# A list scheduler that plans three engines learns of a port that two of them share

## The chip, the cores and the metric

One core of one Trainium2 chip runs the whole program. The metric is the device time of one execution in microseconds, the median of three runs. TensorE is PE in the profile, VectorE is DVE, ScalarE is ACT, GpSimd is POOL, and SyncE (SP) issues the DMAs.

## What is computed

Three layers follow one another, all in float32 (a_re, a_im, q, k, v are 4 x 8 x 768 x 48):

```python
# 1: a linear attention with complex decay, per head, step by step over 768 positions
S_re, S_im = ar * S_re - ai * S_im + k v^T, ar * S_im + ai * S_re
y[t] = q[t] @ S_re
# 2: an MLP 384 -> 2048 -> 384 on 3072 tokens with a rational activation P(h) / Q(h)
g = (a0 + a1*h + a2*h2 + a3*h3) / (1 + |b0|*|h| + |b1|*h2 + 1e-6);  x = g @ w_out
# 3: a mixture of 8 experts 384 -> 1024 -> 384, all tokens through all experts,
#    weighted by P, a softmax normalised 8 times over rows and columns
out += P[:, e:e+1] * (max(x @ w1[e], 0) @ w2[e])
```

## The kernel before

The program has two parts. The **first part** (layers 1 and 2) is a list schedule made at build time; the **second part** (layer 3, `second_mlp`, L1298, and `experts`, L1004) is written out in a fixed order: 384 steps of 9 and 12 matmuls, with one ACT and one DVE instruction between the two.

Layer 1 is cut into 13 pieces. For each piece `attn_normalise` (L345) computes the decay, `attn_prefix` (L385) multiplies it up over the piece (tiles f1a, f2a, u, tot, x, ex), `attn_scale` (L486) scales q and k by it (tiles f1, f2, an, kq) and writes them to a scratch in DRAM, and `attn_unit` and `attn_half` (L534, L582) read them back (tile raw) for 128 tokens at a time, transpose them on PE, multiply and mask them, and give xt, the input of layer 2. Layer 2 works on 12 tiles of 256 tokens and 8 groups of weights: `moe1_first` (L783) does 18 matmuls (h) and the rational function (tiles m, gt, gh, gl) on ACT and DVE, and `moe1_second` (L827) multiplies by the second weights (tile x, results x2s).

Each of these functions is a generator that yields operations. An `Op` (L93) knows its engine, its estimated duration (`cost`) and its inputs: `self.ins` (L101) holds the operands except those that are the very same object as the output. So `scalar_tensor_tensor(out=s1, in0=s1, scalar=c, in1=s3, ...)` of `moe1_first` has s3 and the small c in `ins`, and not s1.

Many two-operand products are an `Either` (`g.tt`): DVE and POOL can both do them, and the planner takes the one with the lower start + cost x (1 + PRICE). With the costs of L93 to L123, a product of 384 columns is 0.468 us on DVE and 0.956 us on POOL.

`Schedule.run` (L300) is the planner. It holds one time per engine at which it is free (`free_at`), finds the operation that can start first, and among the operations of that engine that can start then takes the one whose stream has the earliest due date. It emits that operation and sets the engine's time. The due dates (L1416 to L1430) are multiples of PITCH for each tile of tokens, of GROUP for each group of weights, less a lead for each kind of work: OA for the prefix, ON for the normalising, OB for the scaling, OU for the units, OW for the weights; OS is a lag. All instructions of an engine, and all DMAs of SP's queue, are issued in the order in which the planner emitted them, and semaphores keep the data right, so durations that the planner has wrong change the times on the chip and not the result.

Of the kernel before, what the change touches and what calls it, by code (L numbers as in the profile page):

```python
# [15 lines left out]
PSUM, DRAM = bass.MemoryType.PSUM, bass.MemoryType.DRAM  # L16
# [45 lines left out]
PLAIN = 'FFFSSFFS'  # L62
SMP = 'DD'

PITCH = 52.78
GROUP = 5.87
OU = 61.28
OB = 99.68
OA = 215.64
ON = 87.12  # L70
OW = 36.95
OS = 26.64
SLACK = 0
HHD = 2.38
SH = (-2.5, 27.9, -15.0, 1.6, 3.1, -26.5, 4.2, 13.7, 4.0, 12.5, -36.2, -58.1, 17.9)
WS = 1.91
PRICE = {'DVE': 1.78, 'POOL': 0.13, 'ACT': -0.39}
LAT = {'PE': 0.2, 'ACT': 0.145, 'DVE': 0.13, 'POOL': 0.075, 'SP': 1.0}
TS = True

# [12 lines left out]
class Op:  # L93


    def __init__(self, eng, fn, args, kw):
        self.eng, self.fn, self.args, self.kw = eng, fn, args, kw
        self.deps = []
        self.out = kw["out"] if "out" in kw else args[0]
        ap = [x for k, x in [*enumerate(args), *kw.items()] if k not in ("out", "accum_out", "op", "func") and hasattr(x, "tensor")]  # L100
        self.ins = [x for x in ap if x is not self.out]  # L101
        n = int(np.prod(self.out.shape[1:]))
        ps = any(x.space == PSUM for x in self.ins)
        name = fn.__name__
        ptr = sum(hasattr(kw.get(k), "tensor") for k in ("scale", "bias", "accum_out", "scalar")) + (
            name == "tensor_scalar" and sum(hasattr(x, "tensor") for x in args[2:4]))
        self.lat = LAT[eng]
        if eng == "PE":
            f32 = args[1].dtype != F32R
            two = f32 and not kw.get("is_transpose")  # L110
            self.cost = (1 + two) * max(n * (1 + f32) / 2400, 0.108)
            if two:
                self.cost = {32: 0.076, 96: 0.162}.get(self.out.shape[0], self.cost)
        elif eng == "ACT":
            self.cost = (0.05 if ps else 0.092) + n * 0.836e-3 + 0.0935 * ptr
        elif eng == "DVE":
            one = name == "tensor_scalar" and not ps
            self.cost = ((n / 2 if one else n) + 65) / 960 + 0.061 * ptr
        elif eng == "POOL":
            c = {"tensor_tensor": 2.1, "tensor_scalar": 1.18, "affine_select": 0.9}.get(name, 0.8)  # L120
            self.cost = (0.15 if c > 0.8 else 0.04) + c * n * 1e-3
        else:
            self.cost = 0.06  # L123
# [55 lines left out]
def extent(ap):  # L179

    dims = list(ap.ap)
    o = ap.offset
    if ap.space != DRAM:
        o %= dims[0][0] or 1
        dims = dims[1:]
    return ap.tensor.name, o, o + sum((n - 1) * abs(s) for s, n in dims) + 1


class Schedule:


    def __init__(self, bufs):
        self.bufs = bufs
        self.free_at = dict.fromkeys(("PE", "DVE", "ACT", "POOL", "SP", "DGE", "DMA"), 0.0)
        self.streams, self.seen, self.queues, self.of, self.base = [], {}, {}, {}, {}
        self.log = []

# [13 lines left out]
    def resume(self, s, val):  # L211
        while True:
# [13 lines left out]
            else:  # L226
                if isinstance(x, Either):
                    s.head = [([op], self.ready([op]), op.cost * (1 + PRICE[op.eng])) for op in x.ops]
                else:
# [39 lines left out]
    def ready(self, ops):  # L269
# [7 lines left out]
                        op.deps.append(ix)  # L277
        return r

    def emit(self, s, ops, start):  # L280
        f = self.free_at
        for op in ops:
            if op.eng == "SP":
                f["SP"] = start + op.cost
                t = f["DGE"] = max(f["DGE"], start) + 0.55
                t = f["DMA"] = max(f["DMA"], t + 0.65) + int(np.prod(op.out.shape)) * 4 / 360e3
                end = t + op.lat
                start = f["SP"]
            else:
                end = start + op.cost  # L290
                f[op.eng] = start = end
                end += op.lat
            ins = op.fn(*op.args, **op.kw)  # L293
            self.log.append((op.eng, start - op.cost if op.eng != "SP" else t - 0.5, end, ins, op))
            for ap, w in [(op.out, True)] + [(x, False) for x in op.ins]:
                n, a, b = extent(ap)
                self.seen.setdefault(n, []).append((a, b, end, w, op.eng, len(self.log) - 1))
        self.resume(s, None)

    def run(self):  # L300
        while self.streams:
            go = True
            while go:
                go = False
                for s in sorted((s for s in self.streams if s.wait is not None), key=lambda s: s.key):
                    if s.wait is not None and self.grant(s):
                        go = True
            best = None
            for s in self.streams:
                if s.head is None:  # L310
                    continue
                ops, r, _ = min(s.head, key=lambda h: max(h[1], self.free_at[h[0][0].eng]) + h[2])
                e = ops[0].eng
                t = max(r, self.free_at[e])
                if best is None or t < best[0]:
                    best = t, s, ops, e
            if best is None:
                if self.streams:
                    raise RuntimeError("nothing can go on: " + "; ".join(
                        f"{s.gen.__name__} {s.key:.0f}: {[y.kw['name'] for y in (s.wait if isinstance(s.wait, list) else [s.wait])] if not callable(s.wait) else s.gen.gi_frame.f_lineno}" for s in self.streams)[:400])  # L320
                return
            t0, _, _, e = best
            pick = None
            for s in self.streams:
                if s.head is None:
                    continue
                ops, r, _ = min(s.head, key=lambda h: max(h[1], self.free_at[h[0][0].eng]) + h[2])
                if ops[0].eng != e:
                    continue
                t = max(r, self.free_at[e])  # L330
                if t <= t0 + SLACK and (pick is None or (s.key, t) < pick[0]):
                    pick = (s.key, t), s, ops, t
            self.emit(pick[1], pick[2], pick[3])
# [200 lines left out]
def attn_unit(g, p, u, due):  # L534
# [24 lines left out]
    for hh in range(2):  # L559
        g.add(attn_half(g, n, t0 == 0, last, raw[hh], vt, hh), due + hh * HHD)  # L560
    yield lambda: ("H", n, 0) in g.done and ("H", n, 1) in g.done
# [265 lines left out]
def moe1_second(g, m):  # L827
# [3 lines left out]
    for gi in range(NG):  # L831
        yield lambda: (m, gi) in g.gs and (2 * gi, 1) in g.w1 and (2 * gi + 1, 1) in g.w1
        yield m * PITCH + gi * GROUP + OS
        gh, gl = g.gs.pop((m, gi))
# [451 lines left out]
def x2_load(g, t):  # L1286

    per = TB // TK
    yield lambda: all(("S", t * per + i) in g.done for i in range(per))
    xt = yield New(g.px[t], [128, 2, 3, TB], F32R, keep=True, tag=f"x{t}", name=f"xb{t}")  # L1290
    for l in range(2):
        yield g.eng[4].dma_start(
            out=xt[:, l].bitcast(F32), in_=g.x2g[l, :, :, t * TB:(t + 1) * TB].rearrange("k p t -> p k t")
        )
    g.x2[t] = xt
# [21 lines left out]
def kernel_body(tc, g):  # L1317
# [77 lines left out]
    def tail():  # L1395
# [8 lines left out]
        for t in range(4):  # L1404
            sch.add(x2_load(g, t), PITCH * NT // TK)
        for n in range(8):
            sch.add(expert_entry(g, n), PITCH * NT // TK + n)

    with tc.manual_schedule():
# [4 lines left out]
        for p in range(NP):  # L1414
            b, t0, st = PIECES[p]
            due = PITCH * ((b * S + t0) // TK) + (p == 1) + SH[p]  # L1416
            for hf in range(st // 8):
                sch.add(attn_normalise(g, p, hf), due - ON)
            sch.add(attn_prefix(g, p), due - OA)
            for s in range(st // 4):  # L1420
                sch.add(attn_scale(g, p, s), due - OB)
            for u in range(st // 8):
                sch.add(attn_unit(g, p, u, due - OU + u), due - OU + u)
        for f in range(NF):
            for i in range(2):
                sch.add(moe1_weights(g, f, i), f * WS * GROUP / 2 - OW + i * OS)
        for m in range(NT // TK):
            for gi in range(NG):
                sch.add(moe1_first(g, m, gi), m * PITCH + gi * GROUP)
            sch.add(moe1_second(g, m), m * PITCH + OS)  # L1430
        sch.add(tail(), 0)
# [47 lines left out]
```

## Time and profile before

| | us |
|---|---|
| median of 3 runs (2558.86 to 2560.88) | 2558.94 |
| the profiled execution | 2555.27 |
| its span, first to last instruction | 2553.4 |
| PE busy | 2331.3 |
| DVE busy | 1219.5 |
| ACT busy | 859.3 |
| POOL busy | 662.8 |

The profile page divides the span in 40 slices. In the first 14 of them, some 900 us, all four engines work; in the others PE is busy nearly all the time and the others little. The first matmul `he` of the second part begins at 901 us. An instruction's duration in the profile contains the time in which it has started and cannot get on.

### The profile page before, as it was taken

The page shows a single profiled execution, that of the slowest core. Times are in us where ns is not written, and L with a number is a line of the kernel's source. Part 1 is how long each engine was busy: PE and PEld are TensorE (multiplying, and loading weights), DVE is VectorE, ACT ScalarE, POOL GpSimd, SP SyncE. Part 2 cuts the span into 40 slices and gives each one's busy share as a digit, 9 for nine tenths or more (in the row PEclk, how much of TensorE's full clock was granted, in tenths as well). Part 3 has the DMA queues.
Part 4 walks back from the last instruction along what each step waited for, and adds up shares of the span by engine and source line. Part 5 has one row for each costly group of instructions (what it writes and reads, how often), then busy time and mean ns, then how long its engine had stood idle before and what let it go on. Part 6 is the DMA issues. An engine that isn't in the chain of part 4 may idle for free.

```text
span 2553.4 us, 34934 instructions
## 1 busy us (share of the span) xinstructions
PE 2331.3 (91%) x13921; PEld 2100.8 (82%) x13921; DVE 1219.5 (48%) x2093; ACT 859.3 (34%) x1752; POOL 662.8 (26%) x728
## 2 busy tenths in 40 slices
PE   0468888788899999999999999999999999999998
PEld 0357777777789988999998998998998999999998
DVE  7998989999766633442233224224222222222222
ACT  3456666666667741131121121111112112112111
POOL 5776777777630120020020020011002002001000
PEclk9888999988999999999999999999999999999999
DMA  4533323233320430020021011002001001000000
GB/s 131 161 91 110 95 86 108 86 104 98 107 88 23 155 124 1 1 87 7 1 68 32 1 44 56 1 19 81 1 1 50 1 1 50 1 1 19 25 25 27
DMA packets 141839, 138.20 MB, mean 54 GB/s; under 512 B 32480, under 2 KB 126688, under 8 KB 141664
## 3 DMA queue, kind: packets, MB, share of 16 engines
q1 hardware_dynamic: 141664, 135.86, 17.1%
q8 instruction: 111, 1.82, 0.3%
q14 instruction: 64, 0.52, 0.1%
HBM read 102.80 MB, written 33.03 MB: 53 GB/s over the span
## 4 chain that ended last, share of the span: by engine, by line
PE 71%; DVE 8%; POOL 4%; issue 3%; DMA 2%; ACT 1%; SPq 0%; POOLq 0%; DVEq 0%
PE ye L1035 10%; PE ye L1036 10%; PE he L664 10%; PE ye L1037 10%; PE he L663 10%; PE he L665 10%; PE x L293 4%; PE h L293 3%; DVE m L293 2%; POOL an L293 1%; DVE f L293 1%; POOL kq L293 1%; DVE n L293 1%; DVE f1a L293 1%; ACT m L293 1%
## 5 line engine op out<-in xcount | busy, mean ns | idle before, releaser
L1023 DVE SCALAR_TENSOR_TENSOR lo<-he,hi 128x512 fp32r<-128x512 f32 x384 | 265.4, 691 | 1100.9 <-ACT hi L1022 1100.8
L1022 ACT ACTIVATE hi<-he 128x512 fp32r<-128x512 f32 x384 | 229.7, 598 | 1201.9 <-PE he L665 1055.2
L293 DVE SCALAR_TENSOR_TENSOR m<-m,co,m 128x512 f32<-128x512 f32 x192 | 172.3, 925 | 25.0 <-ACT m L293 24.7
L293 ACT ACTIVATE m<-m,co 128x512 f32<-128x512 f32 x192 | 137.3, 719 | 1.4
L293 PE MATMUL t<-cst_sb,raw 128*96 128x128 f32 x384 | 64.4, 297 | 34.4 <-DMA raw<-kqd 26.8
L1048 DVE SCALAR_TENSOR_TENSOR acc<-ye,skp,acc 128x384 f32<-128x384 f32 x168 | 92.2, 611 | 5.7 <-PE ye L1037 2.4
L293 DVE SCALAR_TENSOR_TENSOR m<-m,co,h 128x512 f32<-128x512 f32 x96 | 71.0, 740 | 34.9 <-ACT m L293 34.7
L293 PEld LDWEIGHTS t<-cst_sb,raw 128*96 128x96 f32 x384 | 46.6, 138 | 43.2 <-issue 24.0
L293 PE MATMUL sh<-tot,cst_sb 128*128 128x96 f32 x26 | 8.1, 408 | 76.4 <-DVE tot L293 73.4
L293 PE MATMUL sc<-tt,tt 96*128 96x128 f32 x384 | 59.7, 304 | 18.9 <-ACT tt L293 17.3
L293 PEld LDWEIGHTS sc<-tt,tt 96*128 96x128 f32 x384 | 53.5, 212 | 24.7 <-ACT tt L293 20.1
L293 POOL TENSOR_TENSOR gl<-m,gh 128x512 fp32r<-128x512 f32 x31 | 44.3, 1431 | 111.2 <-ACT gh L293 111.2
L293 PEld LDWEIGHTS sh<-tot,cst_sb 128*128 128x128 f32 x26 | 5.7, 274 | 79.2 <-POOL tot L293 51.1
L293 ACT ACTIVATE m<-h,co 128x512 f32<-128x512 f32 x96 | 65.4, 681 | 12.3 <-DVE gt L293 6.8
L293 ACT ACTIVATE m<-h 128x512 f32<-128x512 f32 x96 | 56.6, 590 | 32.4 <-PE h L293 32.2
L293 ACT COPY tt<-t 96x512 f32<-96x512 f32 x95 | 54.2, 574 | 28.5 <-PE t L293 28.1
L293 POOL TENSOR_TENSOR f<-an,ex 128x384 f32<-128x384 f32 x51 | 62.5, 1232 | 4.2 <-DVE ex L293 4.1
L293 ACT ACTIVATE m<-m 128x512 f32<-128x512 f32 x96 | 60.2, 628 | 1.3
L293 POOL TENSOR_TENSOR kq<-an,f 128x384 f32<-128x384 f32 x39 | 47.2, 1209 | 36.5 <-DVE f L293 31.3
L293 POOL TENSOR_TENSOR an<-f,f 128x192 f32<-128x192 f32 x61 | 48.9, 811 | 12.8 <-DVE f L293 12.4
L293 DVE SCALAR_TENSOR_TENSOR gt<-m,m 128x512 f32<-128x512 f32 x60 | 50.9, 849 | 2.3 <-PE x L293 0.5
L293 ACT ACTIVATE n<-n,bias 128x384 f32<-128x384 f32 x72 | 43.7, 608 | 10.0 <-POOL n L293 5.9
(1329 smaller groups left out, 7134.6 us busy)
## 6 DMA issues: line engine op xcount, KB each, us to landing
rawe<-in_moe_w SPq DMA_DIRECT2D x128, 192.0 KB
kqd<-kq SPq DMA_DIRECT2D x48, 384.0 KB
raw<-kqd SPq DMA_DIRECT2D x48, 384.0 KB
x2g<-x2s SPq DMA_DIRECT2D x36, 256.0 KB
xb<-x2g SPq DMA_DIRECT2D x12, 768.0 KB
raw<-in_moe_w_in SPq DMA_DIRECT2D x48, 128.0 KB
raw<-in_moe_w_out SPq DMA_DIRECT2D x16, 384.0 KB
rawc<-in_moe_w_in SPq DMA_DIRECT2D x16, 384.0 KB
```

The costliest lines, as they stand in the source:

```text
L293: ins = op.fn(*op.args, **op.kw)
L663: pe.matmul(out, w[0], x[0], start=start, stop=False, **kw),
L664: pe.matmul(out, w[0], x[1], start=False, stop=False, **kw),
L665: pe.matmul(out, w[1], x[0], start=False, stop=stop, **kw),
L1022: act.activation(hi, ps, AF.Relu)
L1023: v.scalar_tensor_tensor(out=lo, in0=ps, scalar=0.0, in1=hi.bitcast(F32), op0=ALU.max, op1=SUB)
L1035: pe.matmul(ys[j], hi[:, c], wh, start=f == 0, stop=False)
L1036: pe.matmul(ys[j], hi[:, c], wl, start=False, stop=False)
L1037: pe.matmul(ys[j], lo[:, c], wh, start=False, stop=f == NFE - 1)
L1048: v.scalar_tensor_tensor(out=acc, in0=ys[j], scalar=g.P[:, i, e:e + 1], in1=acc, op0=MULT, op1=ADD)
```

## The change

The planner gets one more resource, PORT, with a time at which it is free. An operation of POOL that reads SBUF, and an operation of DVE that has two inputs in SBUF or is a `tensor_scalar` or `tensor_copy` from SBUF, starts no earlier than PORT is free, and holds PORT for its whole estimated duration. Inputs are counted from `ins`. The planner's duration of a matmul of rounded operands grows by 0.013 us. PITCH, GROUP, the leads, two of the 13 shifts SH by more than a unit, and the three values of PRICE are new. No operation is added or taken away, pools and buffers stay as they are, and the second part is the same text.

```diff
-PITCH = 52.78
-GROUP = 5.87
-OU = 61.28
-OB = 99.68
-OA = 215.64
-ON = 87.12
-OW = 36.95
-OS = 26.64
+PITCH = 63.96
+GROUP = 6.92
+OU = 52.54
+OB = 77.92
+OA = 199.64
+ON = 97.15
+OW = 45.47
+OS = 27.91
-HHD = 2.38
-SH = (-2.5, 27.9, -15.0, 1.6, 3.1, -26.5, 4.2, 13.7, 4.0, 12.5, -36.2, -58.1, 17.9)
+HHD = 2.39
+SH = (-2.5, 31.7, -15.0, 20.1, 3.1, -26.5, 4.2, 13.7, 4.0, 12.5, -36.2, -58.5, 17.9)
-PRICE = {'DVE': 1.78, 'POOL': 0.13, 'ACT': -0.39}
+PRICE = {'DVE': 1.0, 'POOL': 0.05, 'ACT': -0.18}
...
+        sb = sum(x.space != PSUM and int(np.prod(x.shape[1:])) > 1 for x in self.ins)
+        self.port = sb > 0 and (eng == "POOL" or eng == "DVE" and (sb > 1 or not ps and name in ("tensor_scalar", "tensor_copy")))
...
-            self.cost = (1 + two) * max(n * (1 + f32) / 2400, 0.108)
+            self.cost = (1 + two) * max(n * (1 + f32) / 2400, 0.108) + 0.013 * (not f32)
...
-        self.free_at = dict.fromkeys(("PE", "DVE", "ACT", "POOL", "SP", "DGE", "DMA"), 0.0)
+        self.free_at = dict.fromkeys(("PE", "DVE", "ACT", "POOL", "SP", "DGE", "DMA", "PORT"), 0.0)
...
+    def start(self, h):
+        t = max(h[1], self.free_at[h[0][0].eng])
+        return max(t, self.free_at["PORT"]) if h[0][0].port else t
+
...
                 f[op.eng] = start = end
+                if op.port:
+                    f["PORT"] = end
...
-                ops, r, _ = min(s.head, key=lambda h: max(h[1], self.free_at[h[0][0].eng]) + h[2])
+                h = min(s.head, key=lambda h: self.start(h) + h[2])
+                ops, t = h[0], self.start(h)
```

## Rows read from the trace of the kernel before

**Rows 1.** Five stretches: us; busy PE, PEld, DVE, ACT, POOL; PE's clock; DMA share, GB/s

```profile
0.00:128.00 128.00, 32.53 (x202) 27.02 (x206) 106.75 (x231) 53.87 (x131) 84.21 (x103) 0.90 0.48 146
128.00:448.00 320.00, 252.05 (x2130) 225.21 (x2122) 289.88 (x462) 207.38 (x456) 234.17 (x262) 0.91 0.33 98
448.00:704.00 256.00, 212.18 (x1776) 192.07 (x1777) 225.18 (x382) 160.78 (x352) 179.30 (x208) 0.92 0.32 97
...
768.00:901.00 133.00, 132.88 (x1099) 125.30 (x1099) 86.38 (x125) 96.65 (x189) 18.87 (x15) 1.00 0.25 86
901.00:2553.40 1652.40, 1643.67 (x8196) 1476.75 (x8194) 469.21 (x830) 300.62 (x546) 121.09 (x120) 1.00 0.09 28
```

**Rows 2.** DVE's groups by shape, 128 to 704 us: count, busy us, mean ns, idle before

```profile
L293 DVE SCALAR_TENSOR_TENSOR m<-m,co,m 128x512 f32<-128x512 f32 x124 | 119.0, 983 | 4.3 <-ACT m L293 4.2
L293 DVE SCALAR_TENSOR_TENSOR m<-m,co,h 128x512 f32<-128x512 f32 x62 | 45.7, 737 | 1.5 <-ACT m L293 1.3
L293 DVE SCALAR_TENSOR_TENSOR gt<-m,m 128x512 f32<-128x512 f32 x38 | 35.3, 930 | 0.5 <-DVE m L293 0.5
L293 DVE TENSOR_TENSOR f<-an,ex 128x384 f32<-128x384 f32 x37 | 32.9, 899 | 1.8 <-POOL kq L293 1.8
L293 DVE SCALAR_TENSOR_TENSOR n<-n,n 128x384 f32<-128x384 f32 x38 | 30.5, 803 | 4.8 <-ACT n L293 3.1 <-POOL n L293 1.3
L293 DVE TENSOR_TENSOR f1a<-an 128x384 f32<-128x384 f32 x26 | 25.3, 973 | 1.8 <-POOL an L293 1.8
...
L293 DVE SCALAR_TENSOR_TENSOR f<-f,runs,k 128x192 f32<-128x192 f32 x40 | 21.2, 530 | 5.5 <-ACT f L293 5.4
L293 DVE SCALAR_TENSOR_TENSOR m<-m,m 128x512 f32<-128x512 f32 x23 | 19.7, 855 | 0.0
L293 DVE TENSOR_TENSOR an<-f,f 128x192 f32<-128x192 f32 x27 | 18.7, 700 | 0.0
...
L293 DVE COPY g<-u 96x192 f32<-96x192 f32 x6 | 2.1, 344 | 0.0
L293 DVE TENSOR_TENSOR u<-an 128x96 f32<-128x96 f32 x7 | 1.9, 296 | 1.0 <-POOL an L293 1.0
```

**Rows 3.** Timeline, 564 to 568 us, DVE and POOL: start us, us

```profile
564.14 0.99 POOL L293 TENSOR_TENSOR kq<-an,q 128x384 f32<-128x384 f32 x1
...
565.24 0.68 DVE L293 SCALAR_TENSOR_TENSOR gt<-m,m 128x512 f32<-128x512 f32 x1
...
566.13 0.60 POOL L293 TENSOR_TENSOR f<-f 128x192 f32<-128x192 f32 x1
...
566.70 0.28 POOL L293 TENSOR_TENSOR tot<-u,u 128x48 f32<-128x48 f32 x1
...
566.86 0.20 DVE L293 TENSOR_TENSOR tot<-u,u 128x48 f32<-128x48 f32 x1
566.94 1.00 POOL L293 TENSOR_TENSOR n<-n,n 128x384 f32<-128x384 f32 x1
566.98 1.37 DVE L293 SCALAR_TENSOR_TENSOR n<-n,n 128x384 f32<-128x384 f32 x1
```

**Rows 4.** Timeline, 311 to 314 us, DVE: start us, us

```profile
311.73 0.55 DVE L293 TENSOR_TENSOR kq<-an,q 128x384 f32<-128x384 f32 x1
312.20 0.35 DVE L293 TENSOR_TENSOR f<-f 128x192 f32<-128x192 f32 x1
...
313.16 0.42 DVE L293 SCALAR_TENSOR_TENSOR f<-f,runs,k 128x192 f32<-128x192 f32 x1
```

**Rows 5.** POOL's groups by shape, 128 to 704 us, columns as in rows 2

```profile
L293 POOL TENSOR_TENSOR f<-an,ex 128x384 f32<-128x384 f32 x43 | 53.3, 1248 | 2.8 <-DVE ex L293 2.7
L293 POOL TENSOR_TENSOR an<-f,f 128x192 f32<-128x192 f32 x53 | 42.8, 818 | 12.8 <-DVE f L293 12.4
...
L293 POOL TENSOR_TENSOR x<-u,u 128x48 f32<-128x48 f32 x56 | 26.1, 479 | 41.2 <-DVE u L293 41.2
```

**Rows 6.** PE's longest wait, 0 to 128 us: total us, times, longest

```profile
PE sh L293 <- DVE tot L293: 52.5, 3, 35.4
```

More of the change, by code (lines that the diff above doesn't have):

```diff
@@ L311, in run @@
                     continue
-                ops, r, _ = min(s.head, key=lambda h: max(h[1], self.free_at[h[0][0].eng]) + h[2])
+                h = min(s.head, key=lambda h: self.start(h) + h[2])
+                ops, t = h[0], self.start(h)
                 e = ops[0].eng
-                t = max(r, self.free_at[e])
                 if best is None or t < best[0]:
@@ L326, in run @@
                     continue
-                ops, r, _ = min(s.head, key=lambda h: max(h[1], self.free_at[h[0][0].eng]) + h[2])
+                h = min(s.head, key=lambda h: self.start(h) + h[2])
+                ops, t = h[0], self.start(h)
                 if ops[0].eng != e:
                     continue
-                t = max(r, self.free_at[e])
                 if t <= t0 + SLACK and (pick is None or (s.key, t) < pick[0]):
```

## The prediction

> **What bounds the kernel now.** I read the page first: its slices show four busy engines up to about 900 us and PE alone after that. So I cut the span into stretches [rows 1]. From 901 us on PE is busy 1643.67 of 1652.4 us at full clock; the change does not touch that part, and nothing can be won there. From 768 to 901 us PE is busy 132.88 of 133 us: a backlog of layer 2 is drained. Before that PE is not the bound: it idles 95.5 us in the first 128, and between 128 and 704 us it is busy 464 of 576 us, at a granted clock of 0.91 to 0.92 of 2.4 GHz. In those 576 us DVE is busy 515 and POOL 413. I take DVE, with 61 us idle, as the engine whose pace counts there.
>
> Then I read DVE's groups in that stretch [rows 2]. Two forms of one operation and one size stand side by side: `m<-m,co,h`, one of whose inputs is in PSUM, takes 737 ns; `m<-m,co,m`, with both in SBUF, takes 983. The timeline shows why [rows 3]. A POOL product of 48 columns starts at 566.70 and takes 0.28 us, and DVE meets nothing. At 566.94 POOL starts a product of 384 columns, 1.00 us, at 566.98 DVE starts one, and DVE's takes 1.37 us, where 0.55 us is enough [rows 4]: 0.96 us of POOL, then its own. DVE and POOL take turns at something when both read SBUF.
>
> **How much is waiting.** Own durations by width, unhindered: on DVE 0.55 us for 384 columns, 0.35 for 192, 0.42 for the three-operand one of 192 [rows 4], 0.68 for 512 and 0.20 for 48 [rows 3], 0.737 for the `m` form with a pointer [rows 2]; on POOL 0.99, 0.60 and 0.28 for 384, 192 and 48 [rows 3]. DVE's waits: `m<-m,co,m` 124 x (983 - 737) ns = 30.5 us, `gt` 38 x 250 = 9.5, `f` 37 x 349 = 12.9, `n` 38 x 253 = 9.6, `f1a` 26 x 423 = 11.0, `f<-f,runs,k` 40 x 110 = 4.4, `m<-m,m` 23 x 175 = 4.0, together 82; the 19 smaller groups from `an<-f,f` to `u<-an`, taken the same way, give 70 [rows 2]. So 152 of DVE's 515 us are waiting, 363 its own. Eleven groups with a PSUM input, `m<-m,co,h` to the copy `g<-u`, hold 109 of the 363 (124 by the rows, less 0.057 us for each of 260 instructions: groups overlap by that much). The other 254 us need the shared port. POOL's waits are 43 x 258 ns = 11.1, 53 x 218 = 11.6, 56 x 199 = 11.1 [rows 5], and 57 in its 18 other groups: 91 of 413, so 322 of its own. The two demands, 254 + 322 = 576 us, are as long as the stretch. **The port is taken all the time**; that is the bound.
>
> **What the change moves.** No instruction is added or removed. Three things happen.
>
> First, the planner stops laying two port users over one another, where it sees them. It does not see all. It counts inputs from `ins`, and `ins` leaves out the operand that is also the output, so the in-place DVE forms count one input: `m<-m,co,m` (88 us of its own), `m<-m,m` (16), `f<-f,runs,k` (17), half of `n<-n,n` (10) and some small ones, 126 of the 254 us after overlap. It sees 128.
>
> The row says that these forms wait like the others (983 against 737 ns) [rows 2]. The Trainium skill, page "SBUF — State Buffer", section "Who interferes with whom", says the same against this change: a DVE instruction with two SBUF inputs contends with a GpSimd instruction that reads SBUF, and the second to start is blocked entirely; it makes no exception for an input that is overwritten. If the in-place forms were free, as the plan has it, the sum below would be 64 us of gain and not 42.
>
> Second, work goes from POOL to DVE. With equal starts a product of 384 columns scored 0.468 x 2.78 = 1.30 on DVE against 0.956 x 1.13 = 1.08 on POOL, and POOL took it; now it is 0.94 against 1.00, and DVE does. POOL starts alone only while DVE does something that the plan takes for port-free: 109 + 126 = 235 of 363 us, 65%. So I let POOL keep two thirds: a third, 107 us, goes over and costs DVE 0.55 x 107 = 59 us. (None and all are the ends.)
>
> The new length of the stretch has two bounds. If the port stays full and nothing else limits, it is 254 + 59 + 215 = 528 us, 48 less. If the waits only shrink with POOL's share, to 101 us, and DVE's 61 idle us stay, it is 363 + 59 + 101 + 61 = 584 us, 8 more. The plan then sees (128 + 59) of (254 + 59) us, 60%, and I weigh by that: 0.6 x (-48) + 0.4 x 8 = **-26 us**. In the first 128 us PE's longest wait is for DVE's `tot`, 52.5 us [rows 6], in the same contest (DVE 107, POOL 84 us busy); at the same rate, 128 x 26 / 576, that is **-6 us**, between 0 and twice that.
>
> Third, the dates. In tiles of tokens (leads divided by PITCH) the prefix's lead falls from 4.09 to 3.12, the scaling's from 1.89 to 1.22, the units' from 1.16 to 0.82: attention runs less far ahead, and layer 2 comes earlier in the middle, where PE idles 44 us between 448 and 704. The drain of 133 us, in which DVE has 47 us free and POOL 114 [rows 1], gets shorter by what PE did before. I take a quarter of the 44, **-10 us**, between 0 (layer 2 waits for DVE as before) and -22. The new PE duration changes no matmul, only dates. SP's queue is reordered with the work: a load behind a store of kq that waits for a later kq comes later too. I cost that at nothing, since the DMA engines are a third busy [rows 1] and every lead stays above 45 us; if the cover is gone it is part of the upper end.
>
> **Sum:** -26 - 6 - 10 = -42 us. The profiled execution is 2555.27 us (span 2553.4 and 1.9 around it), 3.7 below the median, so I apply it to the median: 2558.94 - 42 = **2517 us**.
>
> **Rivals.** (a) The plan is too blind. It now puts POOL on purpose beside the in-place `m` forms, which hold the port, so that what the seen forms save is lost again there. For it: half of the demand is unseen. Against it: the plan of before saw none. The 26 and 6 us fall to 0 to 10, the 10 to 0 to 10, and a lost wait adds up to 3: 2535 to 2562 us.
>
> (b) Slower: DVE becomes the bound. With DVE's surcharge cut, everything goes over: 363 + 0.55 x 322 + 61 idle = 601 us, 25 more, and 6 more at the start: 2590 us. It decides from where 177 us x the share moved plus the waits left exceeds 152; at a third moved that is 93 us of waits, at two thirds 34. For it: DVE has only 61 us of slack now. Against it: DVE's waits must go with POOL's work, and as long as DVE is in an operation that the plan takes for free, POOL gets the next product.
>
> (c) The plan's seen half is worth all of the first bound, with half of POOL's work moved: 576 - 0.45 x 161 = 504, 72 us less, and 16 elsewhere: 2471 us. PE then has 464 us of work in 504, which is still less.
>
> **How the numbers follow.** Forecast (2472 to 2535): 0.62; rival (a): 0.20; rival (b): 0.14; beyond (c): 0.04. 0.2%, about 5 us, is what a measurement of this kernel can tell from no change. Of (a) some 0.09 lies below 2554, 0.09 within the 5 us and 0.02 above. Faster: 0.62 + 0.04 + 0.09 = 0.75; same 0.09; slower 0.14 + 0.02 = 0.16. The range 2471 to 2562 holds the forecast and (a), 0.82.
>
> **What would show it.** Right: in the new profile POOL has a fourth to a half fewer two-operand products and DVE that many more; DVE's `f`, `f1a`, `an` and `tot` come down towards 0.55, 0.35 and 0.20 us, while `m<-m,co,m` stays above 0.9; the first `he` comes about 42 us before 901; PE idles less between 128 and 704 us, and the drain before `he` is shorter. The stretch after `he` keeps its 1652 us. Wrong: `m<-m,co,m` rises above 1.1 us (then it is (a)); DVE has over 560 us of its own in the stretch, with POOL mostly idle (then (b)); or PE waits for the tile raw or for loads in place of DVE, which would be the queue.

## The result and the profile after

The changed kernel takes 2520.89 us (median of four runs, 2518.48 to 2526.12) against 2558.90 of the kernel before on the same chip: a ratio of 0.9854, 95% interval [0.9837, 0.9871]. 2517 was forecast, in a range of 2471 to 2562. The profiled execution takes 2521.8 us, its span is 2519.8. The medians differ by 38.0 us and the two profiled executions by 33.5; what follows accounts for the latter. The first matmul `he` of the second part starts at 866.7 us, before at 901.2.

Four stretches, up to that matmul and after it (columns as in rows 1):

```profile
0.00:128.00 128.00, 36.68 (x269) 30.72 (x270) 97.41 (x276) 53.50 (x129) 42.96 (x54) 0.91 0.42 125
128.00:704.00 576.00, 490.87 (x4141) 444.49 (x4140) 512.14 (x980) 387.22 (x843) 288.37 (x326) 0.92 0.34 101
704.00:866.70 162.70, 157.55 (x1323) 146.75 (x1321) 123.25 (x209) 113.85 (x226) 38.60 (x46) 0.99 0.35 112
866.70:2519.80 1653.10, 1643.41 (x8195) 1476.64 (x8193) 468.21 (x834) 299.50 (x544) 113.86 (x113) 1.00 0.09 28
```

The second part keeps its length: 1653.1 us, before 1652.2. All that is gained lies ahead of it. PE's idle time in the first 128 us goes from 95.5 to 91.3; from 128 to 704 us from 111.8 to 85.1; from there to `he` from 6.2 to 5.2; and PE's busy time up to `he` from 687.8 to 685.1. Together 4.2 + 26.7 + 1.0 + 2.7, within rounding the 34.5 us by which `he` comes earlier. POOL is busy 288 us in the long stretch, where it was 413 [rows 1]; DVE starts 980 instructions there, where it was 843, and is busy 512 us, where it was 515.

DVE's groups from 128 to 704 us (count, busy us, mean ns, idle before), to be held against rows 2:

```profile
L302 DVE SCALAR_TENSOR_TENSOR m<-m,co,m 128x512 f32<-128x512 f32 x136 | 119.6, 911 | 7.9 <-ACT m L302 7.9
L302 DVE SCALAR_TENSOR_TENSOR m<-m,co,h 128x512 f32<-128x512 f32 x68 | 49.9, 737 | 0.4 <-ACT m L302 0.3
L302 DVE SCALAR_TENSOR_TENSOR gt<-m,m 128x512 f32<-128x512 f32 x43 | 34.0, 792 | 0.1
L302 DVE TENSOR_TENSOR f<-an,ex 128x384 f32<-128x384 f32 x52 | 32.6, 643 | 0.0
...
L302 DVE SCALAR_TENSOR_TENSOR m<-m,m 128x512 f32<-128x512 f32 x25 | 23.3, 933 | 0.3
...
L302 DVE TENSOR_TENSOR an<-f,f 128x192 f32<-128x192 f32 x36 | 14.2, 405 | 0.0
...
L302 DVE TENSOR_TENSOR f1a<-an 128x384 f32<-128x384 f32 x23 | 12.9, 561 | 0.0
```

And POOL's, against rows 5:

```profile
L302 POOL TENSOR_TENSOR an<-f,f 128x192 f32<-128x192 f32 x36 | 28.3, 789 | 19.6 <-DVE f L302 19.5
L302 POOL TENSOR_TENSOR x<-u,u 128x48 f32<-128x48 f32 x51 | 26.7, 541 | 30.7 <-DVE u L302 30.7
...
L302 POOL TENSOR_TENSOR f<-an,ex 128x384 f32<-128x384 f32 x20 | 24.3, 1222 | 12.6 <-ACT n L302 8.4 <-DVE ex L302 3.6 <-ACT ex L302 0.6
```

The forms that the plan now sees have lost most of their wait (how much of that is due to the plan, the experiments show): `f1a` took 973 ns on average and takes 561, `an<-f,f` 700 and now 405, `f<-an,ex` 899 and now 643. The in-place forms still wait: `m<-m,co,m` 911 ns beside 737 for its twin with a PSUM input, and `m<-m,m` has gone up, from 855 to 933. 136 of the `m<-m,co,m` fit into the stretch and not 124: layer 2 is further on. POOL does `f<-an,ex` 20 times where it did it 43 times, and each still takes 1.2 us.

**An account of the first part.** For every kernel of this study the same sum is made over all instructions of DVE and POOL ahead of the first `he`: for each group of one operation, tiles and shape, its count times its shortest instruction is its own time, and what its instructions took beyond that is waiting. "Port" is the own time of POOL's products and of DVE's forms with two SBUF inputs, in place or not, or with the SBUF form of `tensor_scalar` or copy. Instructions overlap a little, so own time and waiting add up to more than the busy time, and the port's column is an upper figure.

| kernel | instructions in the page, DVE / POOL | port us | DVE own us | DVE waits us | first he at us |
|---|---|---|---|---|---|
| before | 2093 / 728 | 872 | 620 | 209 | 901 |
| changed | 2295 / 537 | 803 | 709 | 120 | 867 |

DVE does 202 instructions more; its own work grows by 89 us, and its waits shrink by as much. The port is needed 69 us less.

### The profile page after: what moved, and what is told of

The parts are those of the page before. It is cut to its first block, busy times and chain, and to the rows that moved or that the text cites. A ratio compares the mean times of both kernels' runs of the same rounds, so it can differ in the third digit from the quotient of the medians.

```text
span 2519.8 us, 34763 instructions
## 1 busy us (share of the span) xinstructions
PE 2328.5 (92%) x13921; PEld 2098.6 (83%) x13921; DVE 1201.0 (48%) x2295; ACT 854.1 (34%) x1741; POOL 483.8 (19%) x537
## 4 chain that ended last, share of the span: by engine, by line
PE 74%; DVE 11%; DMA 6%; issue 3%; POOL 3%; ACT 3%; SPq 1%; POOLq 0%; DVEq 0%; ACTq 0%
PE ye L1044 10%; PE ye L1045 10%; PE ye L1046 10%; PE he L673 10%; PE he L672 10%; PE he L674 10%; PE x L302 4%; DVE m L302 3%; PE h L302 3%; DVE f L302 1%; DMA ai<-in_a_im 1%; ACT m L302 1%; PE t L302 1%; PE sc L302 1%; DVE n L302 1%
## 5 line engine op out<-in xcount | busy, mean ns | idle before, releaser
L302 DVE SCALAR_TENSOR_TENSOR m<-m,co,m 128x512 f32<-128x512 f32 x192 | 165.5, 894 | 18.7 <-ACT m L302 18.5
L302 PE MATMUL t<-cst_sb,raw 128*96 128x128 f32 x384 | 66.5, 304 | 35.6 <-DMA raw<-kqd 33.7
L302 DVE TENSOR_TENSOR f<-an,ex 128x384 f32<-128x384 f32 x70 | 45.5, 665 | 0.0
L302 POOL TENSOR_TENSOR x<-u,u 128x48 f32<-128x48 f32 x62 | 31.6, 526 | 44.6 <-DVE u L302 37.8
L302 POOL TENSOR_TENSOR f<-an,ex 128x384 f32<-128x384 f32 x26 | 32.5, 1256 | 30.7 <-DVE kq L302 10.0
L302 POOL TENSOR_TENSOR kq<-an,f 128x384 f32<-128x384 f32 x21 | 29.9, 1423 | 43.8 <-DVE f L302 26.3
```

## The experiments

Three theories were held against each other. T1: port row and surcharges work together, DVE taking over products and the plan avoiding collisions. T2: the new dates. T3: the surcharges alone. T1 was split later: T1a, the move of products pays; T1b, the knowledge of the port pays. Each ratio is against the kernel before, measured beside that run (medians 2555.7 to 2557.6 us).

**Only the PORT resource.** The diff of the change without its constants and without `+ 0.013 * (not f32)`.

> Only the PORT resource is added to the kernel before; dates, surcharges and the matmul duration stay old. T1 (port row and surcharges work together: the gain is the third of POOL's products that DVE takes, and the collisions that the plan then avoids): with the old surcharges POOL wins every tie at the port (1.08 against 1.30), nearly all products go to POOL, and it is slower than before: about 2600 us, POOL over 900 products. T2 (the new dates are the gain): no change, 2555 to 2563 us. T3 (the surcharges alone are the gain): no change or a few us slower, DVE and POOL sharing the products as before.

Measured: 2645.61 us, ratio 1.0347 [1.0330, 1.0364]: slower by 3.5%, the way T1 had it and by more than the 2600 us that it gave. Two stretches of its profile, columns as above, and POOL's first group:

```profile
0.00:128.00 128.00, 33.25 (x241) 27.47 (x242) 40.77 (x108) 39.99 (x99) 92.47 (x154) 0.92 0.32 94
128.00:704.00 576.00, 408.86 (x3309) 365.84 (x3309) 359.28 (x517) 327.68 (x717) 500.24 (x631) 0.85 0.29 89
```

```profile
L302 POOL TENSOR_TENSOR f<-an,ex 128x384 f32<-128x384 f32 x64 | 73.4, 1154 | 0.0
```

POOL is busy 500 us of 576, DVE 359. By the code of `start`, whenever the port is the last to come free, DVE's start and POOL's start of a product are the same moment, and the surcharges decide the tie: at 1.08 against 1.30 such products go to POOL (1109 instructions in the page, DVE 1713). POOL holds the port for 0.99 us where DVE would for 0.55 [rows 3, 4].

**Only the surcharges.**

```diff
-PRICE = {'DVE': 1.78, 'POOL': 0.13, 'ACT': -0.39}
+PRICE = {'DVE': 1.0, 'POOL': 0.05, 'ACT': -0.18}
```

> Only the three surcharges are new. T1: some products go over to DVE, but blindly, so that the waits stay: 2545 to 2560 us, with DVE's m<-m,co,m still above 0.95 us between 128 and 704 us. T2: no change. T3: the whole gain, about 2521 us.

Measured: 2557.62 us, ratio 1.0005 [0.9996, 1.0015]: no change, as T1 and T2 had it. T3 falls. Without a port in the plan the surcharges move fewer products: 2177 / 664 instructions. T1's sign, `m<-m,co,m` above 0.95 us between 128 and 704 us, was just missed: 0.937.

**The change without the new dates** (PITCH to SH as before).

> The changed kernel with the old PITCH, GROUP, leads and shifts. T1: most of the gain stays, 2525 to 2535 us (about 10 us belong to the dates). T2: no gain is left, about 2559 us. T3: 2521 us.

Measured: 2515.93 us, ratio 0.9836 [0.9820, 0.9852]. The whole gain stays; T2 falls, and so does the share of 10 us that T1 gave to the dates. 2299 / 530 instructions.

**The port seen whole.** Inputs of in-place operations are counted too.

```diff
-        sb = sum(x.space != PSUM and int(np.prod(x.shape[1:])) > 1 for x in self.ins)
+        src = [x for k, x in [*enumerate(args), *kw.items()] if k not in ("out", "accum_out", "op", "func") and not (k == 0 and "out" not in kw) and hasattr(x, "tensor")]
+        sb = sum(x.space != PSUM and int(np.prod(x.shape[1:])) > 1 for x in src)
```

> The changed kernel, but inputs of DVE's in-place operations are counted too, so that the plan sees the whole port. T1: DVE's m<-m,co,m falls from 0.91 us to under 0.80 between 128 and 704 us and POOL gets fewer products; if those waits are what is left of the loss, 2500 to 2512 us. Rival (the plan has DVE idle where it waited): the waits vanish and the time stays at 2515 to 2530 us.

Measured: 2511.37 us, ratio 0.9818 [0.9797, 0.9838]: at the upper edge of what T1 gave, and below the rival's 2515 to 2530. DVE's groups between 128 and 704 us:

```profile
L303 DVE SCALAR_TENSOR_TENSOR m<-m,co,m 128x512 f32<-128x512 f32 x138 | 108.1, 796 | 3.4 <-ACT m L303 3.0
L303 DVE SCALAR_TENSOR_TENSOR m<-m,co,h 128x512 f32<-128x512 f32 x68 | 49.8, 738 | 6.9 <-ACT m L303 6.7
```

With the in-place forms seen, `m<-m,co,m` comes down from 911 to 796 ns. But the plan also gave POOL fewer products (2475 / 354), so this run does not tell seeing from moving.

**The change without the PORT resource.**

```diff
-        self.port = sb > 0 and (...
+        self.port = False and sb > 0 and (...
```

> The changed kernel without the PORT resource; dates, surcharges and matmul duration new. The surcharges alone changed nothing and the dates could be left out, so T1 (port row and surcharges together): the gain is gone, 2550 to 2565 us, DVE doing under 700 of the products. T2 (dates) is out by the earlier run, as is T3; if this one keeps over 25 us of gain, something in the pair of dates and surcharges does it.

Measured: 2562.49 us, ratio 1.0026 [1.0015, 1.0038]. The gain is gone; 2165 / 674 instructions.

**The change with the old surcharges.**

> The changed kernel with the old surcharges. T1: POOL wins every tie at the port and takes over 900 products, 2630 to 2660 us as with the PORT resource alone. If the new dates repair it: under 2600 us.

Measured: 2636.59 us, ratio 1.0311 [1.0288, 1.0334], 1708 / 1108 instructions. As with the port alone.

**Products moved, the plan blind.** The kernel before with one line changed.

```diff
-PRICE = {'DVE': 1.78, 'POOL': 0.13, 'ACT': -0.39}
+PRICE = {'DVE': -0.2, 'POOL': 0.05, 'ACT': -0.18}
```

> No PORT resource, old dates; DVE's surcharge is -0.2 (POOL 0.05, ACT -0.18), so that DVE takes some 750 of the products with no knowledge of the port: two thirds of what the change moved. T1a (moving the products is what pays: 0.44 us of port saved for each of 384 columns): two thirds of the gain, 2528 to 2538 us, waits of DVE falling with POOL's share. T1b (seeing the collisions is what pays; the waits shrink no more than POOL's share while DVE has more to do): 2550 to 2565 us.

Measured: 2519.06 us, ratio 0.9850 [0.9832, 0.9869]: more than T1a expected, the same as the change. 2266 / 605 instructions. So the port in the plan is not needed for the gain.

**The change without the longer matmul in the plan.**

> The changed kernel without the 0.013 us for a matmul of rounded operands. All theories: within 6 us of the changed kernel, 2515 to 2527 us, since no instruction changes its own time and only dates of PE move.

Measured: 2510.45 us, ratio 0.9825 [0.9805, 0.9844], below the expected range; the interval overlaps the changed kernel's.

**Engine and plan taken apart.** The two kernels choose differently for 486 of 1212 operations with a choice. Each choice was written into a table, by function, piece and place in it, and the table given to the other kernel (s.id names the stream, s.nth counts its choices):

```diff
                 if isinstance(x, Either):
+                    e = CHOICE[" ".join(map(str, s.id))][s.nth]
+                    s.nth += 1
+                    x.ops = [op for op in x.ops if op.eng[0] == e]
```

First the changed kernel's engines in the kernel before, whose plan knows nothing of the port:

> The kernel before (no PORT, old dates, old matmul duration), but each product that DVE and POOL (or ACT) can both do is given to the engine that the changed kernel gave it to, from a table. T1a (the move of products pays): at least three quarters of the gain, 2520 to 2530 us, though the plan knows nothing of the port. T1b (knowing the port pays): 2545 to 2560 us.

Measured: 2516.84 us, ratio 0.9842 [0.9825, 0.9859], the whole gain and more than T1a expected. One of the forms that lost their wait in the changed kernel, under this blind plan:

```profile
L339 DVE TENSOR_TENSOR f1a<-an 128x384 f32<-128x384 f32 x24 | 14.5, 604 | 0.0
```

`f1a` takes 604 ns here, 973 before and 561 in the changed kernel; `an<-f,f` 485, 700 and 405; `f<-an,ex` 706, 899 and 643. So most of what these forms lost came with the engines; seeing the port and the new dates account for the smaller part. Then the old engines in the changed kernel, with PORT and new dates:

> The changed kernel (PORT, new dates), but each product is given to the engine that the kernel before gave it to. T1a: a quarter of the gain or less, 2548 to 2560 us. T1b: most of the gain, 2520 to 2535 us.

Measured: 2563.20 us, ratio 1.0025 [1.0015, 1.0035], 3 us above T1a's range. The first of the two runs decides between T1a and T1b: the engines carry the whole gain without any knowledge of the port. The long stretch of both, first the changed engines with the blind plan:

```profile
128.00:704.00 576.00, 489.34 (x4148) 445.20 (x4149) 519.46 (x998) 387.41 (x843) 279.94 (x319) 0.92 0.33 99
```

then the old engines with the plan that knows:

```profile
128.00:704.00 576.00, 455.17 (x3761) 413.55 (x3761) 455.98 (x788) 366.02 (x796) 362.20 (x410) 0.88 0.31 94
```

In the second DVE is busy 456 us where it was 515 [rows 1]: it waits less inside its instructions (156 us in the whole first part, before 209) and it gets to fewer of them (788 in this stretch, before 843). But it is idle for 120 us where it was for 61, and PE does less work than before. Some of DVE's idle time by releaser (before 5.5, 6.4 and 1.9 us), and one wait of PE:

```profile
DVE m L348 <- ACT m L348: 24.7, 30, 2.4
DVE sm L348 <- PE sc L348: 20.9, 14, 6.8
DVE xt L348 <- ACT xt L348: 17.3, 5, 5.6
...
PE x L348 <- ACT w15o L348: 19.5, 1, 19.5
```

The plan keeps DVE and POOL apart as the chip would have done, and what was waiting inside an instruction stands as idle time ahead of it: that is how I read the sums. The port's need, 868 us, is that of before, and so is the time.

This second run is less clean than the first. PE stands still for 19.5 us for one weight, w15o, which is ready at 271 us here and at 178 us in the kernel before; so some gain by the plan may be hidden behind that wait. And the plan sees only half of the port, while the unseen forms collide more than before (983 ns):

```profile
L348 DVE SCALAR_TENSOR_TENSOR m<-m,co,m 128x512 f32<-128x512 f32 x128 | 129.8, 1039 | 14.0 <-ACT m L348 13.3
```

What a plan that sees the whole port would win with the old engines was not measured.

**Nearly all on DVE.** The kernel before with

```diff
-PRICE = {'DVE': 1.78, 'POOL': 0.13, 'ACT': -0.39}
+PRICE = {'DVE': -0.2, 'POOL': 9.0, 'ACT': -0.18}
```

> The kernel before with POOL's surcharge at 9 and DVE's at -0.2, so that DVE does nearly all the products (some 1140, POOL under 70). Rival (b) of the prediction (DVE becomes the bound: 363 + 0.55 x 322 + 61 idle us between 128 and 704): slower than before, about 2590 us. T1a (each product moved saves port time, and without POOL DVE's waits are gone): still faster than before, 2505 to 2530 us.

Measured: 2535.14 us, ratio 0.9911 [0.9894, 0.9928]. Faster than before, slower than the change: between the two expectations. DVE's `m` forms in the whole of this run (shortest, median, longest, ns):

```profile
L293 DVE SCALAR_TENSOR_TENSOR m<-m,co,m x192: 728/745/1512, 123.8 to 877.9; 128x512 f32<-128x512 f32 x192
L293 DVE SCALAR_TENSOR_TENSOR m<-m,co,h x96: 726/741/749, 119.5 to 875.0; 128x512 f32<-128x512 f32 x96
```

Without POOL's products the two twins are alike. Here the port is needed 704 us, less than anywhere, and DVE's own work, 847 us, is the longest of the sums; that it is the bound is argued from that.

**New dates and surcharges for such a share.** The change without the 0.013, and

```diff
-PITCH = 63.96
+PITCH = 69.26
...
-OB = 77.92
-OA = 199.64
+OB = 62.92
+OA = 219.47
...
-PRICE = {'DVE': 1.0, 'POOL': 0.05, 'ACT': -0.18}
+PRICE = {'DVE': 1.0, 'POOL': 0.85, 'ACT': -0.73}
```

with GROUP 6.60, OU 54.46, ON 95.69, OS 32.06, WS (the pace of the weights) 2.07 and three of the shifts SH.

> The changed kernel without the 0.013 us, with dates and surcharges chosen anew so that DVE takes some 970 of the products (DVE 1.0, POOL 0.85, ACT -0.73). T1a (what counts is how long the port is needed, until DVE's own work is as long): the port is needed less than in the changed kernel, as with inplace_seen, and DVE is not yet at the length of all_dve: 2490 to 2512 us, faster than both kernels. Rival (beyond some 800 products on DVE nothing more is to be had): 2508 to 2522 us.

Measured: 2508.46 us, ratio 0.9822 [0.9807, 0.9837], 2449 / 366 instructions. It is the fastest median of the study and faster than the kernel before; its interval and the changed kernel's meet at 0.9837, and from `inplace_seen` and `all_but_pe` it cannot be told apart. Both expectations hold 2508.46, so it does not decide between them.

The account of the first part for all of them, in order of the port's need:

| kernel | DVE / POOL instructions | port us | DVE own us | DVE waits us | first he at us | ratio |
|---|---|---|---|---|---|---|
| all_but_price | 1708 / 1108 | 965 | 481 | 137 | 985 | 1.0311 |
| port_only | 1713 / 1109 | 960 | 484 | 143 | 988 | 1.0347 |
| before | 2093 / 728 | 872 | 620 | 209 | 901 | 1 |
| before_choices | 2093 / 728 | 868 | 616 | 156 | 908 | 1.0025 |
| price_only | 2177 / 664 | 847 | 653 | 199 | 902 | 1.0005 |
| all_but_port | 2165 / 674 | 842 | 658 | 194 | 907 | 1.0026 |
| moved_blind | 2266 / 605 | 815 | 710 | 148 | 865 | 0.9850 |
| all_but_pe | 2271 / 556 | 812 | 691 | 133 | 854 | 0.9825 |
| changed | 2295 / 537 | 803 | 709 | 120 | 867 | 0.9854 |
| after_choices | 2295 / 537 | 801 | 707 | 128 | 862 | 0.9842 |
| all_but_dates | 2299 / 530 | 801 | 712 | 118 | 866 | 0.9836 |
| inplace_seen | 2475 / 354 | 754 | 770 | 76 | 857 | 0.9818 |
| redated | 2449 / 366 | 738 | 772 | 69 | 852 | 0.9822 |
| all_dve | 2664 / 184 | 704 | 847 | 41 | 880 | 0.9911 |

The first part is shorter where the port is needed less, but not in step with it. `price_only` and `all_but_port` need it 25 to 30 us less than before and are no faster; the next 30 us or so, down to `moved_blind`, bring `he` some 40 us forward. Below 815 us little more is won, and in the one run where DVE's own work passes 800 us it turns. In `price_only` PE idles 10 us less than before between 128 and 704 us (101.6, before 111.8), but it works 10 us longer up to `he` (697.9, before 687.8), at a mean granted clock of 0.90 in that stretch, before 0.91; whether the clock is the reason is not shown. In `all_but_port` PE's idle time up to `he` did not fall (215.2, before 213.5).

One rival stands. A product on DVE holds the port for half as long, and it is also done in half the time for whoever waits for it [rows 3, 4]. No run separates the two: that the engines make the gain is shown, that they make it through the port is argued.

## Why the prediction was right, step by step

- **The port is the bound** (254 + 322 = 576 us): near it, but "taken all the time" is too strong. The sum counts whole durations, and port users run side by side at their ends: in rows 3 POOL's `tot` lasts from 566.70 to 566.98, and DVE's `tot`, with two SBUF inputs too, starts at 566.86 and takes its unhindered 0.20 us. The prediction reads this as DVE meeting nothing and then counts both in full. Laid over one another, the rows of all port users of both engines cover 518 of the 576 us, so the port is free for at least 58; in the changed kernel they cover 491. For the bound speaks the run that keeps planner and dates and changes the engines alone: 872 to 801 us of need, and `he` 39 us earlier. Against it speak `price_only` and `all_but_port`.
- **A third of POOL's work goes over**: right in size. Of the 1212 operations with a choice POOL gets 381 and no longer 572 (332 went from POOL to DVE, 131 came back); POOL's own time ahead of `he` goes from 434 to 278 us. The reason given, that ties go to DVE under the new surcharges, is right too, and weighs more than I saw: the same PORT with the old surcharges costs 3.5%. My rivals had no such case, and a forecast that took the PORT row for a gain in itself would have missed the sign of it.
- **The weighing by the share of the port that the plan sees**, 0.6 and 0.4, is the step that failed. Its result, 26 us, was met by luck: PE idles 26.7 us less between 128 and 704 us, but the 10 us of the dates were to come out of the same idle time, 36 in all. And what was weighed, the plan's sight, is not what pays: with new engines and the blind plan the ratio is 0.9842, the changed kernel's is 0.9854; with old engines and the seeing plan it is 1.0025, with the wait for w15o in it. What I called the second bound, waits that shrink with POOL's share, is what happens: POOL's own time falls by 36%, DVE's waits by 39% under the blind plan, by 43% under the changed one. The bound came out at +8 us because it let DVE pay 0.55 us for each product in busy time and kept its idle time. In the first part DVE's own time grew by 89 us and its waits fell by 89; busy time fell from 751 to 733 us all the same, since the 200 more instructions overlap their neighbours, and idle time fell from 151 to 134.
- **The start, -6 us**: 4.2 us. PE's longest wait there hardly moved: 38.1 us, now for POOL's `tot`, before 35.4 for DVE's [rows 6]. It is as long in the other kernels (36.3 us in `redated`), however the port is used. It is the wait of PE's first matmul since the start of the span, and in the changed kernel's chain the load of a_im, issued at 23.48 us, lands only at 32.33; so I was wrong to take it for the contest at the port. What would shorten this chain was not tried.

```profile
PE sh L302 <- POOL tot L302: 38.1, 1, 38.1
```

- **The dates, -10 us**: wrong. With the old dates the gain is at least as large (2515.93 us). The backlog ahead of `he` did get shorter, as forecast: from 704 us to `he` PE works 158 us and no longer 191. But it does so with old dates too, `he` at 866 us: that DVE came to layer 2 earlier because it waited less is argued, not shown.
- **SP's queue, nothing**: PE waits 33.7 us for the tile raw in the whole first part of the changed kernel by its page, 26.8 before; some 7 us that I had at zero. But all idle time ahead of these matmuls went only from 34.4 to 35.6 us, so the term cost little.
- **Rival (a)**, the plan too blind: half right. The in-place forms do go on colliding (`m<-m,m` went up), but the sign named for it, `m<-m,co,m` above 1.1 us, did not come: 0.911. Seeing them changed the time by some 10 us at best (2511 us), and the two intervals touch.
- **Rival (b)**, DVE as the bound at 2590 us: the mechanism exists and is mis-sized. With nearly all products on DVE it is 2535 us. DVE's own time grows about as I had it (620 to 847 us), but with 41 us of waits left, and busy time 758 us, hardly over the 751 of before; I had left the whole of DVE's idle time on top.
- **The rule of the Trainium skill**, page "SBUF — State Buffer", section "Who interferes with whom": the trace agrees that a DVE instruction with two SBUF inputs, in place too, contends with a GpSimd instruction that reads SBUF (911 ns and 796 ns on average for `m<-m,co,m`, a median of 745 where POOL does next to nothing). That the second to start is blocked entirely holds but for the ends: the two `tot` of rows 3 overlap by some 0.1 us, and DVE's is no longer for it. The prediction does not show how its 64 us for free in-place forms are added up; the medians differ by 38.0.

## What to carry to other kernels

When two engines take turns at a port, count how long each would hold it alone. Here, giving work to the engine that does it in half the time made the whole gain, and arranging the turns added nothing that could be seen; with nearly all of the work on that engine, part of the gain was lost again. A planner that learned of half of the turns, with the engines as they were, turned waiting inside instructions into idle time ahead of them. And a shared resource in a greedy planner makes its choices ties: look at the tie-break first, for it decides who does the work.

## What was not expected of the hardware

DVE's instructions run into one another: ahead of `he`, the durations of the kernel before add up to 620 + 209 = 829 us and DVE is busy 751 us; of the changed kernel to 709 + 120 = 829 us, and it is busy 733. That is 78 us for its 1264 instructions up to 901 us and 96 us for some 1465, 0.06 to 0.07 us for each, so that many short instructions on DVE cost less than their rows say.
